# A branch hint for the sync engine ahead of its last branch, and four staging tiles for V instead of two

## The chip, the cores and the metric

The kernel runs on one core of one Trainium2 chip. The metric is the device time of one execution in microseconds (us). TensorE is called PE, VectorE DVE, ScalarE ACT, GpSimd POOL, and SyncE, which issues most transfers, SP. All timed runs of this study with a known state are of state fast, with a granted clock of 0.998 to 1.0 of full speed, so the runs compare directly.

## The reference

Two independent layers run on different inputs, and their outputs are joined along the last axis.

```python
# A: a diagonal state-space scan, L = 2048, D = P = 1024
Bu = einsum('bld,pd->blp', x, B_bar);  h_t = Lam_bar * h_{t-1} + Bu_t
y  = 2 * einsum('blp,dp->bld', h, C).real + x * Dskip
# B: attention with a recurrent memory: 64 segments of 32 rows, 8 memory rows, 32 heads of 128
h = concat([mem, xs]);  q, k, v = h @ Wq, h @ Wk, h @ Wv
o = softmax(mask(q k^T * scale)) v;  o = o @ Wo;  mem = o[:8]
```

The kernel guesses B's memory rows, computes all segments in parallel, and checks the guess at the end. If the check fails, it would run a serial loop, "general". With these inputs it never does, so every engine jumps over that loop. That jump is one of the two subjects here.

## The kernel before

V is made in steps of 4 x 128 rows. Each step's PSUM result is copied into a staging tile and stored from there. Two tiles take turns:

```python
def stage_init(self):
    self.vst = []
    for i in range(2):
        self.vst.append(self.wl.tile([128, 4, 4, EW], BF16, name=f"b_vst{i}", bufs=1))
        self.k.G.memset(self.vst[i][:, :, :, E:EW], 1.0)
    self.nst = 0

def next_st(self):
    self.nst += 1
    return self.vst[self.nst % 2]

def v_x(self, hb, q, w):
    st = self.next_st()
    ...                                   # 4 groups of 8 matmuls; PSUM group P has 3 buffers
    k.copy(..., st[:, i, :, 0:E], p...)   # eviction, nearly always on ACT
    ...
    Q.dma_start(vx[s0:s0 + n * 128, :]..., st[:, 0:n, :, :]...)   # the store, issued by ACT
```

The end of the program, with the hint that PE already had:

```python
def hint(k):
    k.tc.mark_branch_hint_location("general", "LikelyTaken", engines=[mybir.EngineType.PE])
    ...                                   # and keep it where it stands in program order

def out_last(self, ol):                   # the last 128 rows of the output, in three column pieces
    for i, (c0, c1) in enumerate(((0, 512), (512, 768), (768, 1024))):
        ...                               # 32 matmuls, then a copy on DVE, ACT, DVE
        k.SP.dma_start(self.out[0, T - 128:T, D + c0:D + c1], ot[:, c0:c1])

    # in kernel_main, the last blocks of the output projection
    for n, _ in enumerate(b.outproj(tb, ol)):
        if tb == 3 and n == 4:
            hint(k)
    ...
f0 = nc.values_load(b.flag[0:1, 0:1], min_val=0, max_val=1)
with tc.If(f0 == 1, preferred_fallthrough_block=True, label="general"):
    ...                                   # the serial loop; jumped over when the check passes
```

## Time and profile before

| | before |
|---|---|
| time, median of the first three runs | 1246.7 us (1246.66 to 1246.81) |
| span of the profiled run | 1245.3 us |
| PE busy | 1234.2 us, 99% |
| PE's waits, all together | 1.3 us |
| end of the last cast to the end of the span | 5.5 us (1239.74 to 1245.26) |
| SP's branch to SP's first instruction behind it | 2.86 us |

First the head of the page (busy us, share of the span, instructions), and from its part 4 the engines of the chain that ended last:

```profile
PE 1234.2 (99%) x8270; PEld 662.5 (53%) x8342; DVE 667.7 (54%) x1250; ACT 263.4 (21%) x631; POOL 275.8 (22%) x407
...
PE 99%; issue 0%; DVE 0%
```

PE is the whole chain up to the last matmul. A busy PE could still be a slow PE, so the starts are checked in the timeline (start us, length us, engine, line, operation):

```profile
35.74 3.62 PE L64 MATMUL psU<-a_xT,a_bt 128*128 128x512 bf16 x16
39.19 7.07 PE L64 MATMUL psP<-b_wv,b_xe 128*128 128x512 bf16 x31
46.10 3.62 PE L64 MATMUL psU<-a_xT,a_bt 128*128 128x512 bf16 x16
49.55 7.07 PE L64 MATMUL psP<-b_wv,b_xe 128*128 128x512 bf16 x31
```

Read the starts. Sixteen matmuls take 39.19 - 35.74 = 3.45 us, 0.216 us each. The 32 of a V step (31 are recorded, one record is missing) take 6.91 us, also 0.216 us each. There is no room in which PE could be waiting for V.

ACT in the V stage (in brackets: idle us just before, and what ended it):

```profile
29.98 0.37 ACTq L494 DMA_DIRECT2D b_vx<-b_vst  x1
32.54 1.08 ACT L89 ACTIVATE b_vst<-psP 128x512 bf16<-128x512 f32 x2 [1.98 <-PE psP L64]
...
51.48 0.60 ACT L89 ACTIVATE b_vst<-psP 128x512 bf16<-128x512 f32 x1 [4.53 <-DMA b_vx<-b_vst]
```

The eviction at 32.54 us looks as if it had waited for PE. But its matmuls had ended near 30.6 us, and the store of that tile, issued at 25.34, landed at 32.5 by the trace: the tile was the last thing that it waited for. ACT's waits are real, but PE never waits for ACT.

The last part of the program, as the profile lists the instructions of the line with the branch:

```profile
L1156 SPq EVENT_SEMAPHORE  x8: 17/17/17, 1243.0 to 1243.5; - x8
...
L1156 ACTq COMPARE_BRANCH  x1: 58/58/58, 1236.4 to 1236.4; - x1
L1156 ACTq EVENT_SEMAPHORE  x1: 17/17/17, 1236.6 to 1236.6; - x1
L1156 PEldq COMPARE_BRANCH  x1: 418/418/418, 1237.8 to 1237.8; - x1
...
L1156 SPq COMPARE_BRANCH  x1: 58/58/58, 1240.1 to 1240.1; - x1
```

The three numbers are the shortest, middle and longest duration in ns; then come the first and last start. ACT goes on 0.2 us after its branch. SP takes its branch at 1240.1 and does nothing until 1243.0. The list of waits gives that gap to SP itself (total us, times, longest us), and the DMA view of the last 10 us counts the instruction transfers (number, MB, share). Queue q8 carries PE's. Queue q14 carries at least SP's.

```profile
SPq L1156 <- SPq L1156: 2.8, 1, 2.8
```

```profile
q8 instruction: 1, 0.02, 0.9%
q14 instruction: 3, 0.02, 0.7%
```

So, as far as these views show, SP waits for nothing that another engine or a data transfer does. It seems to wait for its own next instruction; the run `e8_last_stores_act` below tests that.

### The profile page before, as it was taken

What the parts mean: (1) busy time and instruction counts of PE and PEld (TensorE: products, weight loads), DVE (VectorE), ACT (ScalarE), POOL (GpSimd) and SP (SyncE); (2) the same over time, 40 slices, a digit from 0 to 9 for tenths busy, and PEclk for the clock granted to TensorE, in tenths of its full rate; (3) what the DMA queues carried; (4) which work ended last, traced back from release to release, by engine and by line L of the source; (5) the groups of instructions that cost most, each with busy time, mean ns of one, the idle gap of its engine ahead of it and who ended that gap; (6) DMA issues with size and microseconds to landing.
All of it is one profiled execution on the core that took longest, in us unless ns stands there. A gap on an engine that the chain in (4) does not pass through costs nothing.

```text
span 1245.3 us, 20124 instructions
## 1 busy us (share of the span) xinstructions
PE 1234.2 (99%) x8270; PEld 662.5 (53%) x8342; DVE 667.7 (54%) x1250; ACT 263.4 (21%) x631; POOL 275.8 (22%) x407
## 2 busy tenths in 40 slices
PE   9999999999999999999999999999999999999998
PEld 5444444444455555556666656555665554446444
DVE  4688899998711124666666666666666641001000
ACT  5344444443310000211112111111211110000000
POOL 4111331212332321322222222222222220000000
PEclk9999999999999999999999999999999999999999
DMA  9965444554898734664454545545553379407000
GB/s 248 272 191 147 131 135 127 144 155 107 242 322 248 249 116 95 196 170 124 96 145 108 144 108 120 132 92 121 120 142 92 65 211 230 107 18 153 17 26 19
DMA packets 316246, 176.83 MB, mean 142 GB/s; under 512 B 138874, under 2 KB 301550, under 8 KB 316150
## 3 DMA queue, kind: packets, MB, share of 16 engines
q1 hardware_dynamic: 294054, 147.95, 47.8%
q10 hardware_dynamic: 21072, 24.38, 5.9%
q0 software_dynamic: 1024, 3.17, 0.7%
q8 instruction: 66, 1.08, 0.4%
q14 instruction: 30, 0.25, 0.1%
HBM read 89.14 MB, written 53.17 MB: 114 GB/s over the span
## 4 chain that ended last, share of the span: by engine, by line
PE 99%; issue 0%; DVE 0%
PE psP L64 82%; PE psU L64 9%; PE psS L64 3%; PE psO L64 2%; PE psR L64 2%; DVE b_xe L91 0%; DVE b_ost L91 0%; DVE a_n L962 0%; DVE hpb L105 0%; DVE ones L102 0%
## 5 line engine op out<-in xcount | busy, mean ns | idle before, releaser
L64 PE MATMUL psP<-b_xe,b_wq 128*128 128x480 bf16 (+1 forms) x1280 | 247.7, 343 | 0.1
L64 PE MATMUL psP<-b_xe,b_wk 128*128 128x480 bf16 (+1 forms) x1280 | 247.7, 343 | 0.0
L64 PE MATMUL psP<-b_wv,b_xe 128*128 128x512 bf16 (+2 forms) x1033 | 223.4, 372 | 0.8
L644 POOL TENSOR_TENSOR b_m<-b_e,maskB 99x396 bf16<-99x396 bf16 x160 | 139.8, 874 | 338.5 <-ACT b_e L641 338.5
L641 ACT ACTIVATE b_e<-psS 99x396 bf16<-99x396 f32 x176 | 88.2, 501 | 536.7 <-PE psS L64 533.4
L64 PEld LDWEIGHTS <-b_wk 128*128 128x128 bf16 x1280 | 119.4, 98 | 94.2
L64 PEld LDWEIGHTS <-b_wq 128*128 128x128 bf16 x1280 | 118.7, 98 | 87.7
L64 PEld LDWEIGHTS <-b_xe 128*128 128x128 bf16 x1056 | 101.8, 98 | 119.1 <-DVE b_xe L91 0.2
L91 DVE CAST b_k<-psP 128x480 bf16<-128x480 f32 (+1 forms) x192 | 97.4, 528 | 100.9 <-PE psP L64 100.9
L91 DVE CAST b_q<-psP 128x480 bf16<-128x480 f32 (+1 forms) x192 | 97.4, 528 | 93.1 <-PE psP L64 91.5
L64 PEld LDWEIGHTS <-b_ol 128*128 128x128 bf16 x864 | 84.3, 98 | 94.4
L64 PE MATMUL psU<-a_xT,a_bt 128*128 128x512 bf16 x493 | 113.9, 379 | 1.1
L64 PE MATMUL psP<-t,a_hl 128*128 128x512 bf16 x496 | 112.1, 379 | 0.8
L91 DVE CAST b_ost<-psP 128x512 bf16<-128x512 f32 (+1 forms) x17 | 11.5, 676 | 177.4 <-PE psP L64 176.3
L64 PE MATMUL psP<-wo,b_ol 128*128 128x512 bf16 (+1 forms) x440 | 91.9, 364 | 0.4
L64 PE MATMUL psP<-t,b_ol 128*128 128x512 bf16 x408 | 91.7, 379 | 0.4
L280 POOL TENSOR_SCALAR a_tt<-a_pr,a_tabf 128x1 f32<-128x1 f32 x48 | 34.1, 710 | 243.2 <-DVE a_pr L275 243.2
L661 DVE TENSOR_TENSOR b_ob<-psO,b_accR 99x384 bf16<-99x384 f32 x160 | 85.9, 553 | 2.4 <-DVE b_accR L660 0.4
L89 ACT ACTIVATE b_vst<-psP 128x512 bf16<-128x512 f32 x126 | 71.9, 589 | 71.3 <-PE psP L64 59.9
L267 DVE TENSOR_TENSOR a_pr<-psU,a_tabf 128x2048 f32<-128x2048 f32 x32 | 73.0, 2282 | 15.7 <-PE psU L64 14.0
L64 PEld LDWEIGHTS <-a_bt 128*128 128x128 bf16 x512 | 49.2, 98 | 57.6
L64 PEld LDWEIGHTS <-a_hl 128*128 128x128 bf16 x512 | 49.0, 98 | 56.7
(200 smaller groups left out, 962.7 us busy)
## 6 DMA issues: line engine op xcount, KB each, us to landing
b_v<-b_vx SPq DMA_DIRECT2D x16, 1122.0 KB
b_wv<-in_B_Wv_dram SPq DMA_DIRECT2D x16, 1024.0 KB
b_vx<-b_vst ACTq DMA_DIRECT2D x24, 544.0 KB
b_on<-b_ob SPq DMA_DIRECT2D x15, 720.0 KB
a_hs<-a_h SPq DMA_DIRECT2D x32, 256.0 KB
b_wog<-in_B_Wo_dram SPq DMA_DIRECT2D x4, 2048.0 KB
b_wq<-in_B_Wq_dram SPq DMA_DIRECT2D x16, 512.0 KB
b_wk<-in_B_Wk_dram SPq DMA_DIRECT2D x16, 512.0 KB
```

Of the source, the lines that this page charges most:

```text
L64: r = f(*a, **kw)
L89: self.S.activation(out, in_, ACT.Copy)
L91: self.V.tensor_copy(out, in_)
L267: V.tensor_tensor(pr[:], u[:].unsqueeze(1).to_broadcast([128, 2, 2, TB]), view(t3, [[TB + 1, 2], [TB + 1, 2], [1, TB]]), ALU.mult)
L280: G.tensor_scalar(tt[:, j:j + 1], w[:, j, TB - 1:TB], t3[:, 1, TB:TB + 1], None, ALU.mult)
L641: k.S.activation(e[:], s[0:GW, :, :, 0:GW], ACT.Exp, scale=float(E) ** -0.5, accum_out=self.accE[0:GW, i:i + 1])
L644: k.G.tensor_tensor(m[0:GW, 0:4 * GP].rearrange("p (a b q) -> p a b q", a=2, b=2)[:, :, :, 0:GW], e[:], mask[0:GW, :, :].unsqueeze(2).to_b ...
L661: V.tensor_tensor(self.ob[:, b0:b0 + n, :], o[0:GW, 0:n, 0:E], r.unsqueeze(2).to_broadcast([GW, n, E]), ALU.mult)
```

## The change

The intent is twofold. SP gets the hint that PE has, so that the target of its jump is fetched ahead. And V's staging gets two more tiles, cut out of the buffer for C (not yet loaded then), so that for the first seven V steps an eviction need not wait for the store of two steps before.

```diff
-    def stage_init(self):
+    def stage_init(self, ct):
...
+        spare = [ct[:, 1, 4 * i:4 * i + 3, :]...[:, 0:16 * EW]... for i in range(2)]
+        self.sts = self.vst + spare
+        for st in self.sts:
+            self.k.G.memset(st[:, :, :, E:EW], 1.0)
...
-        return self.vst[self.nst % 2]
+        return self.sts[self.nst % (4 if self.nst < 8 else 2)]
...
 def hint(k):
-    k.tc.mark_branch_hint_location("general", "LikelyTaken", engines=[mybir.EngineType.PE])
-    ...
+    for e in (mybir.EngineType.PE, mybir.EngineType.SP):
+        k.tc.mark_branch_hint_location("general", "LikelyTaken", engines=[e])
+        ...
```

## The prediction

> **What bounds the kernel.** TensorE. The page gives PE 1234.2 of a 1245.3 us span (99%), the chain that ended last is 99% PE, and the list of waits has a single wait of PE: 1.3 us, for its first operand. In the V stage (10 to 349 us) the timeline shows the 128x512 matmuls back to back, 16 every 3.45 us, 0.216 us each; from 15 us on I find no gap between two starts that is more than a missing record (0.43 us = 2 x 0.216). Nothing that only spares ScalarE or a transfer can shorten the first 1239 us.

> **V staging (two more tiles, in the still empty C buffer, for the first seven V steps).** It removes ScalarE's waits for a store that still reads the tile. The store issued at 25.3 us lands at 32.5, and the eviction that reuses its tile starts at 32.6, about 2 us after its matmuls; the list of waits names 4.5 us more at 51.5. Both are ScalarE's waits. PSUM group P has three buffers, and the late eviction at 32.6 us still frees its buffer about 1 us before PE needs it. Added: two GpSimd memsets of 0.21 us near 4.6 us, ahead of nothing late. The order of PE, DVE and (names apart) ScalarE instructions is unchanged. I expect 0.0 us.

> **The hint.** In the tail, DVE's last cast ends at 1239.8, SP issues the last store at 1239.82, takes its branch at 1240.20 (58 ns), then executes nothing until 1243.06: the list of waits has "SPq L1156 <- SPq L1156 2.8 us". In that gap two instruction transfers of 8 KB run at 1241.39. The store has landed by 1241.55. Other engines resume 0.13 us (ACT) and 0.51 us (DVE) after their branches. So the 2.8 us are a fetch of the branch's target[...]; the trace agrees. After it SP runs eight semaphore waits (0.54 us), then sixteen more instructions and the closing handshake (1.7 us).

> If the hint brings the target in, SP resumes near 1240.35, passes seven waits by 1240.9, waits for the store until 1241.6, and ends at 1243.3: 2.0 us saved. Only about 0.7 us, if the hint brings one page and the closing block lies in the next, fetched at the branch. Nothing, if a hint only steers the next regular page fetch: PE's hint at 1214.5 shows no fetch of its own, only the regular one at 1225.7, and SP seems to have no page boundary left between its hint (about 1212.7) and its branch. The hint itself costs some 45 ns on an idle queue.

> I weigh these 50%, 20%, 30%: 1245.5 us, a gain of 0.1%. Faster by 2% would need 25 us, which the tail does not hold.

> **What would show it.** Hint: SP's 2.8 us wait on itself below 0.5 us, an instruction transfer soon after 1212 us, the end 3.5 us instead of 5.5 us after the last cast. Staging: the ScalarE wait for b_vx near 51.5 us gone, the eviction at 32.6 us up to 1.8 us earlier, the last cast still ending at 1239.8 +- 0.2 us. All of any gain should lie after the last matmul.

> **What would make it wrong.** [...]a different placement of buffers or instructions that moves matmul starts in the first 15 us; ScalarE's earlier stores colliding with the input transposes before 60 us and starving PE.

Two passages are cut above: a rule given as support for the fetch, and a risk. The forecast's sum: 0.5 x 2.0 + 0.2 x 0.7 + 0.3 x 0 = 1.14 us off 1246.7 us, that is 1245.5 us. The 2.0 us follow from the times named in the text. The 0.7 us, given without working, are an estimate; they are near the 0.54 us of the eight waits in the trace of before, which in that case would run during the fetch.

## The result, and the profile after

| | before | after |
|---|---|---|
| median of 4 runs each | 1246.76 us | 1247.02 us (1246.53 to 1247.16) |
| ratio after / before, 95% interval | | 1.0001 (0.9983 to 1.0018) |
| span of the profiled run | 1245.3 us | 1245.4 us |
| end of the last cast to the end of the span | 5.5 us | 5.4 us (1240.01 to 1245.42) |
| SP's branch to SP's first instruction behind it | 2.86 us | 2.75 us |

A ratio here is the mean time of one kernel's fast runs over that of the other's of the same rounds, so it is not quite the ratio of the medians. The two kernels take the same time.

Page and chain after:

```profile
PE 1237.1 (99%) x8342; PEld 661.8 (53%) x8342; DVE 668.4 (54%) x1250; ACT 263.7 (21%) x631; POOL 276.1 (22%) x409
...
PE 99%; DMA 1%; SPq 0%; DVE 0%; issue 0%
```

PE's 2.9 us more are not work: this trace happens to have all 8342 matmul records, the one before lacked 72. POOL has the two added memsets (409 against 407). The timeline of PE after:

```profile
36.02 3.62 PE L64 MATMUL psU<-a_xT,a_bt 128*128 128x512 bf16 x16
39.47 7.07 PE L64 MATMUL psP<-b_wv,b_xe 128*128 128x512 bf16 x32
46.38 3.62 PE L64 MATMUL psU<-a_xT,a_bt 128*128 128x512 bf16 x16
49.83 7.07 PE L64 MATMUL psP<-b_wv,b_xe 128*128 128x512 bf16 x32
```

The starts lie 0.28 us later, and the distances between them are the same to 0.01 us. The shift comes from the first 10 us, where this trace has three short waits of PE for first operands that the trace of before lacks. The first two in time, for `b_xr` and `b_xe`, left no delay: behind them PE was 0.27 us ahead of the trace of before (a start at 8.21 us against 8.48). The 0.28 us appear at the wait for `b_wv` (9.21 against 8.93):

```profile
PE psU L64 <- DMA b_xr<-in_B_x_dram: 0.6, 1, 0.6
PE psP L64 <- DMA b_wv<-in_B_Wv_dram: 0.4, 1, 0.4
PE psP L64 <- ACT b_xe L89: 0.2, 1, 0.2
```

Waits for the same first loads turn up in most of the other runs, with and without the change. Across all profiled runs the last cast starts anywhere between 1238.99 and 1239.59 us, so a difference of 0.3 us at the front says nothing about the change.

ACT after:

```profile
30.26 0.37 ACTq L496 DMA_DIRECT2D b_vx<-t  x1
31.04 0.60 ACT L89 ACTIVATE b_vst<-psP 128x512 bf16<-128x512 f32 x1 [0.20 <-PE psP L64]
...
51.76 0.60 ACT L89 ACTIVATE t<-psP 128x512 bf16<-128x512 f32 x1 [4.52 <-PE psP L64]
```

The eviction that started at 32.54 us now starts at 31.04, in spite of the shift of 0.28. Its wait for the old store is gone. The other wait that the list of before put down to the store (4.53 us, ended at 51.48) is still there, 4.52 us long, and now carries PE's name: the matmuls of that tile had ended last all along. The tile's own store of two steps before, issued at 39.19, had landed by 44.7, and ACT passed the wait for it at 47.76 without delay. What landed near 51.5 was the store issued at 47.34, from the other tile, and the list took that for the cause.

The branch line after, and the hint itself (line 1220):

```profile
L1159 SPq EVENT_SEMAPHORE  x8: 17/17/17, 1243.2 to 1243.7; - x8
...
L1159 PEldq COMPARE_BRANCH  x1: 413/413/413, 1238.0 to 1238.0; - x1
...
L1159 SPq COMPARE_BRANCH  x1: 78/78/78, 1240.4 to 1240.4; - x1
...
L1220 SPq BRANCH_PREFETCH_HINT  x1: 60/60/60, 1212.9 to 1212.9; - x1
```

```profile
SPq L1159 <- SPq L1159: 2.7, 1, 2.7
```

```profile
q14 instruction: 3, 0.02, 0.8%
q8 instruction: 1, 0.02, 0.6%
```

SP executed the hint at 1212.9, 27 us ahead of the branch. The branch took 78 ns instead of 58, so the hint left a trace there. Yet SP still waits 2.7 us, and there are still three 8 KB transfers at the end. No 8 KB transfer runs between the hint and the branch: the hint was issued and nothing was fetched.

### The profile page after: what moved, and what is told of

Read it like the earlier page. It is cut to its first block, busy times and chain, and to the rows that moved or that the text cites. A ratio compares the mean times of both kernels' runs of the same rounds, so it can differ in the third digit from the quotient of the medians.

```text
span 1245.4 us, 20196 instructions
## 1 busy us (share of the span) xinstructions
PE 1237.1 (99%) x8342; PEld 661.8 (53%) x8342; DVE 668.4 (54%) x1250; ACT 263.7 (21%) x631; POOL 276.1 (22%) x409
## 4 chain that ended last, share of the span: by engine, by line
PE 99%; DMA 1%; SPq 0%; DVE 0%; issue 0%
PE psP L64 83%; PE psU L64 9%; PE psS L64 3%; PE psO L64 2%; PE psR L64 2%; DMA b_wv<-in_B_Wv_dram 1%; SPq L64 0%; DVE b_ost L91 0%
## 5 line engine op out<-in xcount | busy, mean ns | idle before, releaser
L89 ACT ACTIVATE b_vst<-psP 128x512 bf16<-128x512 f32 x110 | 63.0, 589 | 58.3 <-PE psP L64 55.4
```

The costliest lines, as they stand in the source:

```text
L89: self.S.activation(out, in_, ACT.Copy)
```

## The experiments

Theory A: a hint on SP only redirects SP's next regular instruction fetch. The instruction transfers that fit SP (8 KB, at 122, 382, 640 and 897 us, with 81, 211, 333 and 465 recorded SP instructions ahead of them in the trace of before, so about 128 apart) put the last one at 897 us and, by this count, the next turn of a page near instruction 593, within a few instructions of the branch (588 ahead of it). By a page is meant here what one such transfer brings; that SP goes by such pages is my estimate from this count. The changed kernel's hint at 1212.9 comes 316 us after the one and too close to the other.

In the tables, "gap" is the time from the start of SP's branch to the start of its first instruction behind it, "tail" is the time from the end of the last cast to the end of the span, and medians are in us.

### The parts alone: `e1_hint_only`, `e2_staging_only`

`e1_hint_only` is the kernel before with only the second half of the diff, `e2_staging_only` with only the first.

> The kernel before with only the SP hint added. Theory A (a hint only steers the sequencer's next regular page fetch, and SP has none left between 1212.7 us and its branch): nothing changes, 1246.7 us within 0.4, SP's 2.8 us wait behind its branch stays, two 8 KB instruction transfers after the branch. Rival B (the hint works alone and the staging tiles cost about 2 us in the changed kernel): about 1244.7 us.

> The kernel before with only the four staging tiles. Theory A: 1246.7 us within 0.4, ScalarE's wait for b_vx near 51.5 us gone, matmul starts from 15 us to the last cast unchanged within 0.2 us. Rival B: about 1248.7 us.

| run | ratio to before (95%) | median | before in these rounds | gap | tail |
|---|---|---|---|---|---|
| e1_hint_only | 0.9998 (0.9981 to 1.0015) | 1246.77 | 1246.88 | 2.71 | 5.4 |
| e2_staging_only | 0.9998 (0.9981 to 1.0015) | 1246.77 | 1246.88 | 2.71 | 5.4 |

No gain is hidden behind a loss. Each part is worth nothing by itself, as theory A and the reading of PE's stream expect, and rival B falls.

### An earlier hint for SP: `e4_sp_hint_early`

```diff
 for n, (hp, u) in enumerate(at):           # the attention loop, 16 x 11 steps
     ...
+    if hp == 11 and u == 0:
+        hint(k, [mybir.EngineType.SP])
     ...
         if tb == 3 and n == 4:
-            hint(k)                        # PE and SP
+            hint(k, [mybir.EngineType.PE])
```

> The changed kernel with SP's hint moved forward to about 850 us, ahead of what I take for SP's last regular page fetch (the 8 KB instruction transfer at 896.9 us; SP's fetches lie 128 instructions apart at 122, 382, 640 and 897 us). Theory A: that fetch brings the branch's target, SP's 2.8 us wait behind the branch falls below 0.5 us, and the kernel takes 1244.7 us (or about 1246.0 us, if the closing block lies in a second page). Rival D (a hint on SP does nothing, wherever it stands, or is forgotten before the branch): 1246.7 us and the 2.8 us wait as before.

Measured: 1244.65 us (1244.45 to 1244.86), ratio 0.9982 (0.9965 to 0.9998). Gap 0.54 us, tail 3.3 us (1239.42 to 1242.75).

```profile
L1161 SPq EVENT_SEMAPHORE  x8: 17/17/17, 1240.4 to 1241.0; - x8
...
L1161 SPq COMPARE_BRANCH  x1: 78/78/78, 1239.8 to 1239.8; - x1
...
L1222 SPq BRANCH_PREFETCH_HINT  x1: 60/60/60, 842.6 to 842.6; - x1
```

```profile
q8 instruction: 1, 0.02, 0.6%
q14 instruction: 2, 0.02, 0.5%
```

The same hint, 370 us earlier, does what the change was meant to do: one transfer fewer at the end and 2.2 us off the median of before in the same rounds (1246.88). No extra transfer appears at 842 us. Between the hint and the branch the 8 KB transfers are the same seven as in the changed kernel (here at 868.5, 895.2, 918.1, 939.4, 970.9, 1031.6 and 1120.4 us), so if a transfer brought the target, it was one of these, and by the count only the one at 895 is SP's (no view names what a transfer brings). The two that remain at the end start 1.2 to 1.3 us after DVE's branch and after SP's.

### On either side of the page fetch: `e5_sp_hint_past_turn`, `e9_sp_hint_behind_turn`, `e11_sp_hint_just_behind`

The same edit with the hint at other steps of the attention loop (`hp == 12 and u == 1`, `hp == 13 and u == 2`, `hp == 12 and u == 2`).

> The early SP hint moved from 842 us to about 912 us, just past the page fetch at 896 us that brought the target in the run with the early hint. If what counts on SP is a page fetch between hint and branch (theory A), the target is not fetched: SP's wait of 2.7 us behind its branch is back and the kernel takes 1246.7 us. If what counts is only the distance in time to the branch (rival E: 28 us is too short, 330 us is enough), or if SP like PE fetches a target at once when the hint comes past the last page fetch (rival C, which PE's late hint showed: a transfer 1.2 us behind the hint), 1244.65 us; with rival C an 8 KB instruction transfer about 913 us that the other runs do not have.

> The run e5 did not test what it was for: SP's queue runs ahead, its hint was executed at 873 us, still ahead of the page fetch at 895 us. Here the hint comes behind that fetch, about 930 us, 310 us ahead of the branch. Theory A (SP's hint is used by the next regular page fetch only, and there is none): SP's 2.7 us wait behind the branch is back, 1246.8 us. Rival E (enough distance to the branch is what counts): 1244.65 us. Rival C (a fetch at once, as PE's late hint made at 1229.3 us): 1244.65 us and a new 8 KB instruction transfer about 931 us.

> PE's late hint (e3) started a transfer of its own 3.8 us behind PE's page fetch, while SP's hints 34 us and 316 us behind SP's page fetch started none. Here SP's hint comes within about 5 us of SP's page fetch at 896 us. If a hint right behind a page turn is still taken (theory G, the same rule for both engines): a new 8 KB transfer about 901 us and 1244.65 us. If SP takes a hint only at its next regular page fetch (theory A as it stands for SP, and PE is different): no new transfer, SP's 2.7 us wait, 1246.9 us.

| run | hint executed at, us | ratio to before (95%) | median | gap |
|---|---|---|---|---|
| e4 (above) | 842.6 | 0.9982 (0.9965 to 0.9998) | 1244.65 | 0.54 |
| e5 | 873.7 | 0.9988 (0.9971 to 1.0004) | 1245.27 | 0.54 |
| (SP's page fetch) | (about 895 to 897) | | | |
| e11 | 899.9 | 1.0002 (0.9986 to 1.0017) | 1247.06 | 2.75 |
| e9 | 934.3 | 1.0001 (0.9984 to 1.0018) | 1246.99 | 2.73 |
| changed kernel | 1212.9 | 1.0001 (0.9983 to 1.0018) | 1247.02 | 2.75 |

The run e5 failed as an experiment. SP's queue runs ahead of the loop, so its hint came at 873.7 us, still ahead of the fetch and not behind it, and its name is wrong. It says only that 873.7 works as 842.6 does. The runs e9 and e11 did what e5 was for. Between 873.7 and 899.9 us the effect is lost at once, and of the seven transfers only the one at 895 us lies there. In all these runs SP has the same 590 recorded instructions ahead of its branch, so a moved page boundary is not the cause. Distance to the branch (rival E) would need its limit between 340 and 366 us (e11 and e5), just where the page fetch lies. That is not excluded outright, but nothing else speaks for it. In neither e9 nor e11 did the late hint start a transfer of its own (the expectation of e11 says 34 us behind the fetch for e9; it was 37). From the traces of e9 and of e11:

```profile
L1161 SPq EVENT_SEMAPHORE  x8: 17/17/17, 1243.1 to 1243.6; - x8
...
L1222 SPq BRANCH_PREFETCH_HINT  x1: 60/60/60, 934.3 to 934.3; - x1
```

```profile
L1161 SPq EVENT_SEMAPHORE  x8: 17/17/17, 1243.0 to 1243.6; - x8
...
L1222 SPq BRANCH_PREFETCH_HINT  x1: 60/60/60, 899.9 to 899.9; - x1
```

### Moving the page turn instead of the hint: `e6_pad_hint`, `e7_pad_no_hint`

```diff
         if tb == 3 and n == 4:
             hint(k)                        # e6: PE and SP, as in the changed kernel; e7: PE alone
+            pad = k.drp.tile([12, 128], BF16, name="pad")
+            for r in range(12):            # twelve stores that nobody needs
+                tc.keep_in_program_order(nc.sync.dma_start(pad[r:r + 1, :], k.ident[0:1, :]))
```

> The changed kernel, with its hint where it was (1212.7 us), and twelve stores of one row to a scratch tensor on SP's queue directly behind the hint, so that SP's next page turn (which I count to fall within two instructions of the branch) comes into the stores, between 1213 and 1220 us, some 20 us ahead of the branch. Theory A: an 8 KB instruction transfer appears there, it is the target, SP's wait behind the branch is below 0.5 us and the kernel takes 1244.65 us. Rival E (distance in time): 1246.8 us, the wait stays 2.7 us.

> The same twelve stores in the kernel before, without a hint on SP: the control for the stores. Theory A: the page fetch falls there too, but brings the next page in sequence; SP waits 2.7 us behind its branch, 1246.7 us within 0.4. If the stores alone (a moved page boundary) brought the gain: 1244.65 us.

Measured: e6 1245.17 us (ratio 0.9987, 0.9970 to 1.0004), e7 1245.0 us (ratio 0.9985, 0.9968 to 1.0001). Gaps 0.55 and 0.53 us, tails 3.6 us both. The intervals of the ratios (as those of e5 and e10) just include 1; the gaps and the tails are what tells these runs from before.

The control gained as much as the test, so e6 says nothing about the hint, and my expectation for e7 was wrong. In e7, without any hint on SP, the branch hits:

```profile
L1159 SPq EVENT_SEMAPHORE  x8: 17/17/17, 1240.8 to 1241.7; - x8
...
L1159 SPq COMPARE_BRANCH  x1: 58/58/58, 1240.2 to 1240.2; - x1
```

One 8 KB transfer now falls between 1213 and 1220 us, where the kernel before has none:

```profile
q14 instruction: 1, 0.01, 0.3%
```

So a transfer came where I had counted the page turn, and behind it SP's gap is 0.53 us instead of 2.86, with two 8 KB transfers at the end instead of three. From this and from the count I infer that this transfer brought the target without any hint, and that the miss of the kernel before comes from where its instructions fall between two transfers. No view names what a transfer brings, so that is not shown. What was measured is that twelve idle stores ahead of the branch cure the miss nearly as well as a hint does (tail 3.6 us against 3.3).

### SP leaves early: `e8_last_stores_act`

```diff
-            k.SP.dma_start(self.out[0, T - 128:T, D + c0:D + c1], ot[:, c0:c1])
+            (k.SP if i == 0 else k.nc.scalar).dma_start(...)     # the last two stores on ACT
```

> The kernel before, with no hint on SP, but the last two stores issued by ScalarE, so that SP takes its branch at about 1233.6 us and its missing page can be fetched while PE still works. If the 2.8 us behind the branch is the fetch and nothing else in the closing sequence costs them (theory A), SP is through its fetch at 1236.5 us, waits for the last store until about 1241.6 us and the kernel takes 1244.7 us as with the early hint. If the 2.8 us were a wait for the last store or for another engine (rival F), it moves with the end: 1246.7 us.

Measured: 1244.72 us (1244.52 to 1244.80), ratio 0.9982 (0.9966 to 0.9999). The miss is still there, 2.97 us long, but from 1233.5 us on, while PE works:

```profile
L1156 SPq EVENT_SEMAPHORE  x8: 17/17/17, 1236.5 to 1241.4; - x8
L1156 SPq COMPARE_BRANCH  x1: 58/58/58, 1233.5 to 1233.5; - x1
```

The miss keeps its length when the end of the kernel is far away, and it is free when it is taken early. Rival F falls. This trace also tells apart the 8 KB transfers of the end, which in before lie at 1241.34, 1241.37 and 1243.58 us. Here one runs 1.0 us after SP's branch (1234.51) and one 0.55 us after SP goes on (1237.02), so these two are SP's. The third, at 1241.33, comes 7.8 us after SP's branch and 1.4 us after DVE's (1239.97).

### PE's own hint: `e3_pe_hint_late`, `e10_early_hint_no_pe_hint`

`e3_pe_hint_late` is the kernel before with PE's hint at `n == 6` instead of `n == 4`. `e10_early_hint_no_pe_hint` is the kernel before with SP's early hint and without PE's.

> The kernel before with PE's own hint moved from about 1214.5 us to about 1228 us, that is behind PE's last regular page fetch at 1225.7 us. Theory A: the hint comes too late, PE's branch at 1237.8 us misses, PE's first wait behind it (1239.4 us before) moves to about 1240.6 us, with no instruction transfer between 1228 and 1237 us; the kernel's time stays at 1246.7 us, for SP ends later still. Rival C (a hint starts a fetch at once): a 16 KB transfer on PE's instruction queue about 1229.5 us, and PE passes its branch as before.

> The kernel before (two staging tiles) with SP's hint at about 842 us and with PE's own hint taken out. If the staging tiles have no part in the gain and PE's branch is off the end's path: 1244.65 us as with four tiles and both hints, SP passes its branch in about 0.5 us; PE, now without a hint, misses at 1237.1 us and makes its first wait behind the branch at about 1239.9 to 1240.1 us instead of 1238.7, ahead of SP's closing (1241.6 us). If the staging tiles matter: more than 1245.5 us. If PE's miss reaches the end: up to 1246 us.

In e3 (one look, 1246.82 us) theory A was wrong for PE. The hint came at 1228.3 us, behind PE's page fetch at about 1225.7. PE's branch still took 417 ns, and a transfer shows between 1227 and 1232 us that the kernel before does not have:

```profile
q8 instruction: 1, 0.02, 1.7%
```

In e10 (1245.1 us, ratio 0.9987, 0.9970 to 1.0003; SP's gap 0.54 us) PE's branch shows what the hint had been saving PE:

```profile
L1156 PEldq COMPARE_BRANCH  x1: 3377/3377/3377, 1237.8 to 1237.8; - x1
...
L1156 PEldq EVENT_SEMAPHORE  x1: 51/51/51, 1241.2 to 1241.2; - x1
```

So 3377 ns instead of about 417. PE is through at 1241.2 us, over 1 us later than I had expected, yet still just ahead of SP's last wait at 1241.4. PE's miss therefore hides behind the last store. With SP cured there is next to no room left for it.

### The smallest version that gains: `e12_two_tiles_early_hint`

This is the kernel before (two tiles, PE's hint as it was) with the early SP hint of e4 as the only addition.

> The smallest version that should beat both kernels: the kernel before with PE's hint where it was and SP's hint at about 842 us, no further staging tiles. 1244.65 us, 2.1 us and 0.17% under the kernel before, the same as the run e4 with four tiles. If the four tiles had a part in e4's gain: above 1245.5 us.

Measured over five rounds: 1244.67 us (1244.53 to 1245.37) against 1246.76 us, ratio 0.9983 (0.9970 to 0.9997). Gap 0.53 us, tail 3.3 us. This beats both kernels by about 2 us with one instruction and no added tiles.

## Why the prediction was right or wrong

- **No difference near 2%: right, in part by luck.** It said a gain of 0.1%, and that 2% is out of reach. The ratio is 1.0001. Any of its three cases for the hint would have fitted, for all lie within 2.0 us, or 0.2%, of the kernel before, and the case that it favoured did not come. The point, 1245.5, was 1.5 us too low. It is a mean of the three cases (about 1244.7, 1246.0 and 1246.7 us) and stands for none of them.
- **Staging worth 0.0 us: right.** The runs with and without it agree (e2 against before, e12 against e4), and PE's starts keep their distances. The eviction at 32.54 us came 1.5 us earlier, as far as said. One reading was wrong: "the ScalarE wait for b_vx near 51.5 us gone" is true of the name only. The 4.5 us stayed and belong to PE.
- **The 2.8 us are a fetch of the branch's target: right, as far as the traces show.** SP's gap was 2.66 to 2.97 us whenever the branch missed and 0.53 to 0.55 us when it did not; in e4, e7, e10 and e12, where it did not, two 8 KB transfers run at the end instead of three. In e8 the gap keeps its length (2.97 us) far from the end, with an 8 KB transfer inside it (1234.51 us). That this transfer brings the target is inferred. The end of the hit runs came 3.3 to 3.6 us after the last cast, near the prediction's 3.5.
- **The step that failed is the weight: "I weigh these 50%, 20%, 30%".** The third case held, "Nothing, if a hint only steers the next regular page fetch". The term of 2.0 us for the hint measured nothing in the changed kernel (the gap went from 2.86 to 2.75, but it is 2.71 in e2 and 2.66 in e3 without any hint on SP) and 2.1 us where the hint was early enough (e12). Part of the evidence was on the table: the trace of before shows PE's hint without a transfer of its own, though e3 later showed that a late hint on PE does make one. The count of SP's instructions between its page fetches, done before predicting, would have put SP's last fetch at 897 us.
- **A detail read wrongly:** "two instruction transfers of 8 KB run at 1241.39", both taken for SP's. The hit runs still show two on that queue at the end. By their times, 1.15 to 1.4 us after DVE's branch and 1.0 to 1.3 us after SP's, one of the pair is DVE's. The run e8 bears it out: with SP's branch 6.5 us ahead of DVE's, SP's transfers move with it and one stays behind DVE's. The trace itself does not name the engine.

What stays open: PE's late hint (e3, at 1228.3 us) started a 16 KB transfer about 1.2 us later, SP's late hints (899.9, 934.3, 1212.9) never did. On SP a hint 3 us behind the page fetch (e11) was no better than one 316 us after it. Whether the difference lies in the engine, in the size of its pages or in where the target lies was not tried. Nor does any view name the page that a transfer brings: that the fetch at 895 us carried the target in e4 is concluded from the missing transfer and the missing stall.

## What to carry to other kernels

When one engine is 99% busy, look for the rest behind its last instruction: there, 2.1 us of a stall were had here for one instruction (e12), while buffers added in the middle gave nothing (e2). On SP the hint had to come ahead of the last regular page fetch (here some 340 us and about 125 recorded instructions before the branch); on PE it did not have to (e3). So look for the instruction transfers in the trace before placing a hint, and look for a missing one after. SP needed no hint at all once it could take its last branch early, because ACT issued the last stores (e8).
